# w_out loaded by column halves, and the first MoE2 chunk computed by column halves

## The chip, the cores and the metric

The kernel runs on one core of a Trainium2 chip. The metric is the device time of one execution in microseconds (us); lower is better.

## What is computed

Sliding-window attention with a linear bias, then a two-layer network with the activation h cos h:

```python
B, H, S, D = 8, 8, 576, 64                 # q, k, v: [B, H, S, D]
scores = q @ k^T / sqrt(D)
bias   = -slope[head] * |i - j|            # kept where 0 <= i - j < 128
x   = softmax(scores + bias) @ v           # as [B*S, H*D] = [4608, 512]
h   = x @ w_in                             # w_in  [512, 2048]
out = (h * cos(h)) @ w_out                 # w_out [2048, 512]
```

Inputs and output are float32 in HBM; inside, the kernel works in bfloat16 with float32 sums. Loads issued by GpSimd convert on the way, so that the sizes of loads in the profile are those of the bfloat16 that is written.

## The kernel before

The 4608 tokens are cut into nine chunks of 512 (`NCH` = 9). For a chunk, **MoE1** (`moe1`, L760) makes h in 16 feature blocks of 128 (`fc`): four matmuls each, a cosine on ScalarE (L765) and a product on VectorE (L769) that gives the tile `gT`. In chunk 0 the first blocks go by parts of 128 or 256 tokens (`moe1_part`, L784). **MoE2** (`moe2`, L813) then makes the output: for each of four token tiles of 128 rows, 16 matmuls over the feature blocks with 512 columns of `w_out` as the moving operand, summed in one PSUM bank. It has the two banks `OB` = [0, 1] in turn. ScalarE or VectorE copies the bank to `ob` (L820, L821), and SyncE's queue stores it (L825).

Between them runs the **attention** of the next tokens, in units: block 0 of a batch, then three blocks by two groups of heads, then a last block of 64. A unit has scores (L569), an exponential (L596), a mask on VectorE (L615), the product with V (L631 to L645), a division (L668 to L682), and the way into `xT`, which is the input of MoE1: by TensorE transposes (L722) or by a transposing DMA on SyncE's queue (L744, L747). After MoE1 of chunk 0, units 7 to 14 are due, in pairs: the last of batch 0 and seven of batch 1. The queries and keys of batches 0 and 1 are transposed on TensorE (L510), the later ones by DMAs on SyncE's queue (L412, L415).

**The loads** are issued by GpSimd (L384 q and k, L392 V, L403 later q and k, L424 w_in, L431 w_out), in the order in which they are written down. They pass through one queue, so that a load lands behind those issued before it. At the start that order is: rows of q and k, V of batch 0 and w_in, mixed; `qend` and `kend`, the last 64 tokens of batch 0's q and k; the last quarter of w_in; q and k of batch 1; the last V of batch 0; w_out in four pieces; V of batch 1 in five; then q and k of batch 2 in five pieces each (`qnat`, `knat`).

**The order on every engine** comes from a planner (`Plan.schedule`). Each operation is written with the time that it occupies its engine (`occ`), the time until its result is there (`lat`), a priority (`pri`, low goes first) and the keys that it reads and writes. For a load `lat` is the time that it takes on the wire, and the planner adds these up in the queue's order:

```python
wire = max(wire, st + 2300) + o.lat
o.end = max(wire, st + o.occ + 1400) + 500
```

From these times it writes out, before the kernel is built, which operation stands behind which on each engine; on the chip each engine follows that order and waits on semaphores. On TensorE an operation with a priority below 5 (scores, products with V, transposes) is taken when it can start; otherwise the one that can start first, and of those the lowest priority (MoE1 has 5, MoE2 has 6) and the earliest written:

```python
near = [(st, o) for st, o in cand if st <= soon]
return min(near, key=lambda c: (c[1].pri, c[1].seq))
```

A matmul of MoE2 reads the key `("wo", u)` of its piece of w_out: before the change piece u holds the rows of feature blocks 4u to 4u + 3 with all 512 columns.

Of the kernel before, what the change touches and what calls it, by code (L numbers as in the profile page):

```python
# [7 lines left out]
ACTF = mybir.ActivationFunctionType  # L8
# [3 lines left out]
B, H, S, D = 8, 8, 576, 64  # L12
# [5 lines left out]
NFC = DFF // 128  # L18
# [268 lines left out]
def bass_alibi_sliding__then__act_gcu_kernel(  # L287
# [8 lines left out]
    with ExitStack() as ctx:  # L296
# [4 lines left out]
        op = R.op  # L301
# [64 lines left out]
        def load_qk(which, src, b, n=0):  # L366
            t0, rr, _ = PIECES[b][n]
            c0 = 64 * (t0 // 32)
            rows = bass.AP(src.tensor, src[b].offset + 64 * t0,
                           [[64 * rr, 32], [64 * S, H], [1, 64 * rr]])  # L370
            if b == 0 and n == 0:
                op("sp" if which == "q" else "act", [lambda e: e.dma_start(qF[which][:, :, :], rows)],
                   w=[("qF", which)], dma=f"ld{which}f", occ=700 if which == "q" else 2000,
                   lat=4000 if which == "q" else 3300, pri=0)
                i = qF[which][:, :, :].rearrange("p y (j d) -> p y j d", j=4)
                o = qC[which][:, :, :, :].rearrange("p j y d -> p y j d")
                op(("act", "dve"),
                   {"act": lambda e: e.activation(o, i, ACTF.Copy),
                    "dve": lambda e: e.tensor_copy(o, i)},
                   r=[("qF", which)], w=piece_keys(which, b, n), occ={"act": 460, "dve": 330},  # L380
                   lat={"act": 560, "dve": 410}, pri=2)
                return
            o = qE[which][:, :, :] if t0 == 512 else qB[which][:, :, c0:c0 + 64 * rr]
            op("pool", [lambda e: e.dma_start(o, rows)],  # L384
               w=piece_keys(which, b, n), dma=f"ld{which}{n}", occ=750,
               lat={2: 600, 4: 800 if which == 'q' else 900,
                    8: 2600 if which == 'q' else 1300, 18: 2850}[rr])

        def load_v(b, order=range(NBLK), behind=()):
            for t in order:  # L390
# [32 lines left out]
        def load_w_in(f0, f1):  # L423
            op("pool", [lambda e: e.dma_start(  # L424
                w_in[:, :, 256 * f0:256 * f1],
                moe_w_in[:, 256 * f0:256 * f1].rearrange("(k p) c -> p k c", p=128))],
               w=[("wi", f) for f in range(f0, f1)], dma=f"wi{f0}", occ=750,
               lat=1300 * (f1 - f0))

        def load_w_out(u):  # L430
            op("pool", [lambda e: e.dma_start(  # L431
                w_out[:, 4 * u:4 * u + 4, :],
                moe_w_out[512 * u:512 * u + 512, :].rearrange("(f p) j -> p f j", p=128))],
               w=[("wo", u)], dma=f"wo{u}", occ=750, lat=2600)

        def constants():
            op("dve", lambda e: e.memset(zeros[:, :], 0.0), w=["zeros"], occ=60, pri=0)
# [364 lines left out]
        def moe2(c):  # L802
            gi = c % 2
            for t in range(4):
                tg = 4 * c + t
                last = tg == 4 * NCH - 1
                row = CH * c + 128 * t
                for n, (j0, j1) in enumerate([(0, 384), (384, 512)] if last else [(0, 512)]):
                    bank = OB[(tg + n) % 2]
                    oi = (tg + n) % NOB  # L810
                    w = j1 - j0
                    for fc in range(NFC):
                        op("pe", lambda e, t=t, fc=fc, bank=bank, j0=j0, j1=j1: e.matmul(  # L813
                            ps[:, bank, 0:j1 - j0], gT[gi][:, fc, 128 * t:128 * t + 128],
                            w_out[:, fc, j0:j1], start=(fc == 0), stop=(fc == NFC - 1)),
                           r=[("g", gi, fc, t), ("wo", fc // 4)], w=[("B", bank)],
                           occ=w * 427 // 1024 + 3, lat=w * 427 // 1024 + 166, pri=6)
                    o, i = ob[oi][:, 0:w], ps[:, bank, 0:w]
                    op(("act", "dve"),
                       {"act": lambda e, o=o, i=i: e.activation(o, i, ACTF.Copy),  # L820
                        "dve": lambda e, o=o, i=i: e.tensor_copy(o, i)},  # L821
                       w=[("B", bank), ("ob", oi)],
                       occ={"act": 70 + 420 * w // 512, "dve": 70 + 536 * w // 512},
                       lat={"act": 170 + 420 * w // 512, "dve": 155 + 536 * w // 512}, pri=6)
                    op("sp", [lambda e, o=o, row=row, j0=j0, j1=j1: e.dma_start(  # L825
                        out[row:row + 128, j0:j1], o)],
                       r=[("ob", oi)], dma=f"st{oi}", occ=350, lat=0)

        ucount = [0]

# [74 lines left out]
        load_qk("q", q, 1)  # L905
        load_qk("k", k, 1)
        load_v(0, [4])
        for u in range(4):
            load_w_out(u)
        load_v(1)  # L910
        next_t, next_v = 2, 2
        for c in range(NCH):
            if c == 0:
# [22 lines left out]
            while next_t < B and done >= 8 * (next_t - 1):  # L936
# [4 lines left out]
                if next_t < B:  # L941
                    load_nat("q", q, next_t)
                    load_nat("k", k, next_t)
            moe2(c)
        R.schedule(filler=lambda e: e.matmul(ps[:, UB[1], 0:128], zeros[:, :],
                                             zeros[:, :], start=True, stop=True),
                   fill=(900, 8300))
# [29 lines left out]
```

## Time and profile before

| | |
|---|---|
| median of 3 runs | 309.34 us (309.11 to 309.60) |
| the profiled execution | 309.74 us |
| its span, first to last instruction | 307.9 us |
| granted TensorE clock, mean | 1.00 |
| TensorE busy | 299.7 us |
| ScalarE, VectorE busy | 199.9, 194.1 us |

Times in the rows below are microseconds from the start of the span. PE is TensorE's matmuls, PEld its weight loads, DVE VectorE, ACT ScalarE, POOL GpSimd, SP SyncE; a q behind it is the engine's own queue. A row of the timeline has the start, the length, the engine and line, the operation, what it writes and reads, its shape and count; in brackets stands the idle time ahead of it and what ended it. A matmul's length is longer than its distance from the next, since they are pipelined. A row of the stages has the stretch, its length, and the busy time (instructions) of PE, PEld, DVE, ACT and POOL, then clock, DMA share and GB/s. A row of DMA issues has the kind, the count, the bytes written and the time from issue to landing. Some matmul records are missing from the trace.

### The profile page before, as it was taken

What the parts mean: (1) busy time and instruction counts of PE and PEld (TensorE: products, weight loads), DVE (VectorE), ACT (ScalarE), POOL (GpSimd) and SP (SyncE); (2) the same over time, 40 slices, a digit from 0 to 9 for tenths busy, and PEclk for the clock granted to TensorE, in tenths of its full rate; (3) what the DMA queues carried; (4) which work ended last, traced back from release to release, by engine and by line L of the source; (5) the groups of instructions that cost most, each with busy time, mean ns of one, the idle gap of its engine ahead of it and who ended that gap; (6) DMA issues with size and microseconds to landing.
All of it is one profiled execution on the core that took longest, in us unless ns stands there. A gap on an engine that the chain in (4) does not pass through costs nothing.

```text
span 307.9 us, 6411 instructions
## 1 busy us (share of the span) xinstructions
PE 299.7 (97%) x2556; PEld 157.4 (51%) x2600; DVE 194.1 (63%) x402; ACT 199.9 (65%) x268; POOL 97.0 (32%) x122
## 2 busy tenths in 40 slices
PE   8899999999999999999999999999999999999996
PEld 6685555445554555445544554455445554444444
DVE  6687777574668566856785568656966588742000
ACT  6888854885488746873688378746964588752211
POOL 8997201355055505550348023900500000000000
PEclk9999999999999999999999999999999999999999
DMA  9999999999399979999699959995991420001112
GB/s 148 173 204 207 207 162 203 140 162 181 105 127 130 170 122 141 129 168 106 155 122 156 151 109 150 165 179 96 169 106 44 113 70 0 0 0 70 68 73 97
DMA packets 150332, 39.08 MB, mean 127 GB/s; under 512 B 138912, under 2 KB 145312, under 8 KB 150304
## 3 DMA queue, kind: packets, MB, share of 16 engines
q0 software_dynamic: 100688, 18.10, 80.6%
q1 hardware_dynamic: 49344, 20.33, 33.2%
q8 instruction: 20, 0.33, 0.5%
q10 hardware_dynamic: 272, 0.26, 0.3%
q14 instruction: 8, 0.07, 0.1%
HBM read 36.70 MB, written 9.44 MB: 150 GB/s over the span
## 4 chain that ended last, share of the span: by engine, by line
PE 83%; DMA 7%; POOL 5%; ACT 2%; issue 1%; DVE 1%; POOLq 0%; ACTq 0%
PE ps L813 37%; PE ps L760 36%; DMA w_outb<-in_moe_w_out_dram 7%; PE ps L569 5%; ACT p L596 2%; PE ps L643 2%; PE ps L645 2%; POOL vp L392 1%; PE ps L631 1%; POOL w_inb L424 1%; POOL qrows L384 1%; POOL krows L384 1%; PE ps L635 1%; DVE p L615 1%; POOL w_outb L431 0%
## 5 line engine op out<-in xcount | busy, mean ns | idle before, releaser
L813 PE MATMUL ps<-w_outb,gT 128*128 128x512 bf16 (+2 forms) x566 | 132.8, 373 | 2.6 <-issue 1.1
L760 PE MATMUL ps<-xT,w_inb 128*128 128x512 bf16 x528 | 120.9, 379 | 0.9 <-issue 0.2
L769 DVE TENSOR_TENSOR gT<-ps,cos 128x512 bf16<-128x512 f32 x136 | 90.3, 688 | 21.1 <-ACT cos L765 16.3
L765 ACT ACTIVATE cos<-ps,halfpi 128x512 f32<-128x512 f32 x136 | 90.0, 688 | 18.9 <-PE ps L760 13.9
L596 ACT ACTIVATE p<-ps 128x1024 bf16<-128x1024 f32 x64 | 61.7, 1023 | 33.3 <-PE ps L569 33.3
L760 PEld LDWEIGHTS ps<-xT,w_inb 128*128 128x128 bf16 x544 | 52.0, 98 | 59.5 <-ACT p L596 0.6
L813 PEld LDWEIGHTS ps<-w_outb,gT 128*128 128x128 bf16 x592 | 53.2, 98 | 56.4 <-DMA w_outb<-in_moe_w_out_dram 1.7
L392 POOL DMA_DIRECT2D vp<-in_v_dram x40 | 33.7, 867 | 88.4 <-DMA xT<-xnat 68.9
L615 DVE TENSOR_TENSOR p<-p,emask 128x1024 bf16<-128x1024 bf16 x58 | 39.1, 682 | 26.8 <-ACT p L596 26.7
L820 ACT ACTIVATE ob<-ps 128x512 f32<-128x512 f32 (+2 forms) x21 | 12.1, 576 | 41.8 <-PE ps L813 35.3
L403 POOL DMA_DIRECT2D qnat<-in_q_dram x30 | 25.3, 876 | 23.1 <-DMA qt<-qnat 23.1
L403 POOL DMA_DIRECT2D knat<-in_k_dram x30 | 25.3, 874 | 11.1 <-DMA kt<-knat 8.3
L682 DVE TENSOR_TENSOR xnat<-ps,rec 128x256 bf16<-128x256 f32 x48 | 19.8, 420 | 1.3
L821 DVE COPY ob<-ps 128x512 f32<-128x512 f32 x16 | 10.9, 683 | 15.1 <-PE ps L813 15.1
L569 PE MATMUL ps<-qt,kt 64*128 64x128 bf16 (+1 forms) x576 | 19.4, 211 | 0.4 <-DVE qt L526 0.2
L569 PEld LDWEIGHTS ps<-qt,kt 64*128 64x128 bf16 x576 | 14.5, 94 | 9.7 <-issue 4.5
L643 PEld LDWEIGHTS ps<-vp,p 128*128 128x128 bf16 x192 | 14.2, 97 | 9.0 <-issue 6.1
L643 PE MATMUL ps<-vp,p 128*128 128x65 bf16 x192 | 17.4, 193 | 0.2 <-ACT xT L731 0.2
L645 PE MATMUL ps<-vp,p 128*128 128x65 bf16 x192 | 17.5, 193 | 0.0
L645 PEld LDWEIGHTS ps<-vp,p 128*128 128x128 bf16 x192 | 13.2, 97 | 2.3
L680 DVE RECIPROCAL rec<-ps 128x4 f32<-128x4 f32 x48 | 8.2, 176 | 6.3 <-PE ps L645 5.8
L631 PEld LDWEIGHTS ps<-vp,p 128*128 128x128 bf16 x128 | 7.3, 97 | 3.6 <-issue 1.8
(66 smaller groups left out, 150.0 us busy)
## 6 DMA issues: line engine op xcount, KB each, us to landing
out_dram<-ob SPq DMA_DIRECT2D x35, 256.0 KB, 2.2
vp<-in_v_dram POOLq DMA_DIRECT2D x32, 128.0 KB, 7.1
qnat<-in_q_dram POOLq DMA_DIRECT2D x24, 128.0 KB, 6.6
knat<-in_k_dram POOLq DMA_DIRECT2D x24, 128.0 KB, 5.1
w_outb<-in_moe_w_out_dram POOLq DMA_DIRECT2D x4, 512.0 KB, 21.9
w_inb<-in_moe_w_in_dram POOLq DMA_DIRECT2D x3, 512.0 KB, 12.8
qrows<-in_q_dram POOLq DMA_DIRECT2D x1, 576.0 KB, 15.6
krows<-in_k_dram POOLq DMA_DIRECT2D x1, 576.0 KB, 17.7
```

The source lines that it names most:

```text
L392: op("pool", [lambda e, t=t, rows=rows: e.dma_start(vp[b % 2][0:rows, t, :, 0:64], v[b, :, 128 * t:128 * t + rows, :].rearrange("h p d -> ...
L403: fns.append(lambda e, t=t, rows=rows: e.dma_start(nat[which][0:rows, t, :, :], src[b, :, 128 * t:128 * t + rows, :].rearrange("h p d -> p ...
L569: ins = e.matmul(ps[:, banks[x], c0:c0 + n_], keys_ap(b, x, pr, kc), query_ap(b, x, pr, qb, n_), start=not acc, stop=stop)
L596: op("act", lambda e: e.activation(P[i][:, 0:1024], ps[:, banks[0]:banks[0] + 2, :].rearrange("p a b -> p (a b)"), ACTF.Exp, scale=0.125), ...
L615: op("dve", lambda e: e.tensor_tensor(p, p, m, ALU.mult), r=[("P", i), ("EM", 0), ("EM", 1)], w=[("P", i)], occ=600, lat=690, pri=1)
L643: e.matmul(o, P[i][:, c0:c0 + 128], V[:, qb - 1, h, 0:65], start=True, stop=False)
L645: ins = e.matmul(o, P[i][:, c0 + 128:c0 + 256], V[:, qb, h, 0:65], start=False, stop=True)
L682: op("dve", lambda e: e.tensor_tensor(o, U[:, :, :, 0:64], rv[:, :, :, None].broadcast_to([128, 2, 2, 64]), ALU.mult), r=[("rec", n % 4)], ...
L760: op("pe", lambda e, kc=kc: e.matmul(ps[:, bank, :], w_in[:, kc, 128 * fc:128 * fc + 128], xT[:, kc, r0:r0 + CH], start=(kc == 0), stop=(k ...
L765: op("act", lambda e: e.activation(cosb[ci][:, :], ps[:, bank, :], ACTF.Sin, bias=halfpi[:, 0:1]), r=["halfpi"], w=[("B", bank), ("cos", c ...
L769: op("dve", lambda e: e.tensor_tensor(gT[gi][:, fc, :], ps[:, bank, :], cosb[ci][:, :], ALU.mult), r=[("cos", ci)], w=[("B", bank)] + [("g ...
L813: op("pe", lambda e, t=t, fc=fc, bank=bank, j0=j0, j1=j1: e.matmul(ps[:, bank, 0:j1 - j0], gT[gi][:, fc, 128 * t:128 * t + 128], w_out[:, ...
```

## The change

w_out is loaded in four pieces again, but each has half of the columns and half of the rows: pieces 0 and 1 are columns 0 to 255 for feature blocks 0 to 7 and 8 to 15, pieces 2 and 3 the same for columns 256 to 511. V of batch 1 is loaded between the second and the third piece. MoE2 of chunk 0 is written by column halves (`moe2_first`): for each half the four token tiles in the order 0, 2, 1, 3, with 16 matmuls of 256 columns each. Tiles 0 and 1 share bank 0, tiles 2 and 3 bank 1, one in each half of it. A full bank is copied out at once and stored as 256 rows by 256 columns. The other chunks keep `moe2`, where a matmul now waits for both column halves of its rows. Planned times of loads that are not otherwise changed are lowered: `qend` and `kend` from 600 to 370 ns, q and k of batch 1 from 2850 to 2790, w_in from 1300 to 1275 for each 256 columns. The time planned for issuing a piece of w_out goes from 750 to 900.

```diff
-               lat={2: 600, 4: 800 if which == 'q' else 900,
-                    8: 2600 if which == 'q' else 1300, 18: 2850}[rr])
+               lat={2: 370, 4: 800 if which == 'q' else 900,
+                    8: 2600 if which == 'q' else 1300, 18: 2790}[rr])
...
-               lat=1300 * (f1 - f0))
+               lat=1275 * (f1 - f0))
 
         def load_w_out(u):
+            f0, j0 = 8 * (u % 2), 256 * (u // 2)
             op("pool", [lambda e: e.dma_start(
-                w_out[:, 4 * u:4 * u + 4, :],
-                moe_w_out[512 * u:512 * u + 512, :].rearrange("(f p) j -> p f j", p=128))],
-               w=[("wo", u)], dma=f"wo{u}", occ=750, lat=2600)
+                w_out[:, f0:f0 + 8, j0:j0 + 256],
+                moe_w_out[128 * f0:128 * f0 + 1024, j0:j0 + 256].rearrange(
+                    "(f p) j -> p f j", p=128))],
+               w=[("wo", u)], dma=f"wo{u}", occ=900, lat=2600)
...
-                           r=[("g", gi, fc, t), ("wo", fc // 4)], w=[("B", bank)],
+                           r=[("g", gi, fc, t), ("wo", fc // 8), ("wo", 2 + fc // 8)], w=[("B", bank)],
...
+        def moe2_first():
+            for y in range(2):
+                j0 = 256 * y
+                for t in (0, 2, 1, 3):
+                    for fc in range(NFC):
+                        op("pe", lambda e, t=t, fc=fc, j0=j0: e.matmul(
+                            ps[:, OB[t // 2], 256 * (t % 2):256 * (t % 2) + 256],
+                            gT[0][:, fc, 128 * t:128 * t + 128], w_out[:, fc, j0:j0 + 256],
+                            start=(fc == 0), stop=(fc == NFC - 1)),
+                           r=[("g", 0, fc, t), ("wo", 2 * y + fc // 8)], w=[("B", OB[t // 2])],
+                           occ=109, lat=275, pri=6)
+                for n, bank in enumerate(OB):
+                    oi = 2 * y + n
+                    o = ob[oi][:, :]
+                    i = ps[:, bank, :]
+                    op(("act", "dve"),
+                       {"act": lambda e, o=o, i=i: e.activation(o, i, ACTF.Copy),
+                        "dve": lambda e, o=o, i=i: e.tensor_copy(o, i)},
+                       w=[("B", bank), ("ob", oi)], occ={"act": 490, "dve": 606},
+                       lat={"act": 590, "dve": 691}, pri=6)
+                    o = out[256 * n:256 * n + 256, j0:j0 + 256].rearrange("(t p) j -> p t j", p=128)
+                    i = ob[oi][:, :].rearrange("p (t j) -> p t j", t=2)
+                    op("sp", [lambda e, o=o, i=i: e.dma_start(o, i)],
+                       r=[("ob", oi)], dma=f"st{oi}", occ=400, lat=0)
...
-        for u in range(4):
-            load_w_out(u)
+        load_w_out(0)
+        load_w_out(1)
         load_v(1)
+        load_w_out(2)
+        load_w_out(3)
...
-            moe2(c)
+            moe2_first() if c == 0 else moe2(c)
```

## The prediction

> **What bounds the kernel now.** I read the page first: the busy line, the granted clock and the chain that ended last.
>
> ```profile
> span 307.9 us, 6411 instructions
> PE 299.7 (97%) x2556; PEld 157.4 (51%) x2600; DVE 194.1 (63%) x402; ACT 199.9 (65%) x268; POOL 97.0 (32%) x122
> PEclk9999999999999999999999999999999999999999
> PE 83%; DMA 7%; POOL 5%; ACT 2%; issue 1%; DVE 1%; POOLq 0%; ACTq 0%
> ```
>
> TensorE is busy for 97% of the span at full granted clock, so only its idle time can be won, and work added to it is paid. The one large share of the chain that is not TensorE's is 7% of DMA. The table by stages says how much idle time there is around the change, and the chain in order of time says what the 7% is:
>
> ```profile
> 54.00:300.00 246.00, 243.47 (x1872) 121.21 (x1908) 155.39 (x304) 159.36 (x211) 65.89 (x79) 1.00 1.10 115
> 34.40:54.05 19.65, 18.73 (x216) 10.31 (x219) 13.11 (x34) 11.89 (x17) 1.33 (x2) 1.00 1.90 188
> ```
> ```profile
> 16.56 22.84 DMA w_outb<-in_moe_w_out_dram
> ```
>
> The first number after the comma is TensorE's busy time. In the stage in which MoE2 of chunk 0 runs it is idle for 19.65 - 18.73 = 0.92 us; in all of 54 to 300 us for 2.5 us. A gain above 0.9 us has no source in this stage. The chain passes through the third piece of w_out, which lands at 39.40: up to there TensorE waits on the load queue, from there on it only works. TensorE's timeline shows the same:
>
> ```profile
> 34.44 1.89 PE L813 MATMUL ps<-w_outb,gT 128*128 128x512 bf16 x8
> 36.42 0.63 PE L569 MATMUL ps<-qt,kt 64*128 64x64 bf16 x24
> 36.98 1.90 PE L813 MATMUL ps<-w_outb,gT 128*128 128x512 bf16 x8
> 39.45 1.04 PE L813 MATMUL ps<-w_outb,gT 128*128 128x512 bf16 x4 [0.56 <-DMA w_outb<-in_moe_w_out_dram]
> 54.04 13.98 PE L760 MATMUL ps<-xT,w_inb 128*128 128x512 bf16 x63
> ```
>
> Eight matmuls of the first piece (two token tiles by four row blocks), the scores of two units, eight of the second piece, then 0.56 us of idle until the third. From 39.45 to 54.04, where chunk 1's MoE1 begins, no wait is left that matters. So the number to find is: when does the last wait for w_out end after the change, and how much MoE2 work is left then? All before that wait is hidden by it; all behind it is paid.
>
> **When the pieces land.** Issues on GpSimd's queue, and time to landing of the four pieces of w_out in order and of the first piece of V behind them:
>
> ```profile
> 15.08 2.99 POOL L431 DMA_DIRECT2D w_outb<-in_moe_w_out_dram  x4
> 18.03 4.24 POOL L392 DMA_DIRECT2D vp<-in_v_dram  x5
> ```
> ```profile
> w_outb<-in_moe_w_out_dram POOLq DMA_DIRECT2D x1, 512.0 KB, 19.2
> w_outb<-in_moe_w_out_dram POOLq DMA_DIRECT2D x1, 512.0 KB, 21.0
> w_outb<-in_moe_w_out_dram POOLq DMA_DIRECT2D x1, 512.0 KB, 22.8
> w_outb<-in_moe_w_out_dram POOLq DMA_DIRECT2D x1, 512.0 KB, 24.8
> vp<-in_v_dram POOLq DMA_DIRECT2D x1, 128.0 KB, 24.9
> ```
>
> The issues are 0.75 us apart, so the pieces land at 34.3, 36.83, 39.4 and 42.1, and V at 42.9: one queue, in order, 2.54 us for a piece of w_out and 0.8 for 128 KB of V. Nothing ahead of w_out is changed, so its first piece still starts at 31.74.
>
> A piece after the change is as many bytes, but 1024 rows of 512 bytes as written in place of 512 rows of 1024. What the packets cost, from two stretches of the trace: one in which the queue moves the 512-byte rows of q and k (4.3 to 5.3 us), one in which it moves w_out (32 to 38 us):
>
> ```profile
> DMA packets 385, 0.19 MB, mean 187 GB/s; under 512 B 26, under 2 KB 385, under 8 KB 385
> DMA packets 1246, 1.24 MB, mean 207 GB/s; under 512 B 36, under 2 KB 1246, under 8 KB 1246
> ```
>
> Without the small ones that is 359 packets of 512 bytes a us (352 on this queue, which I take) against 1210/6 = 202 of 1024 bytes. A new piece takes 1024/352 = 2.91 us, an old one 512/202 = 2.54: 0.37 us more for each. The second piece, with which the first column half is complete, lands at 36.83 + 2 x 0.37 = 37.57.
> The Trainium skill says in DMA: Bandwidth & Descriptors, under Specifications, that transfers of 512 bytes and more run at line rate. By that the second piece would land at 36.83 and the sum below come out at 0.0; the 187 against 207 GB/s of the two rows disagrees. The same page of the Trainium skill, under Why small descriptors are slow, gives every packet about 3 cycles beside one for each 32 bytes: 2 x 19 / 35, an estimate of 9% more time, and a sum of about +0.4 us; the two rows have 15%.
>
> **Part by part.** First, what the order makes of it. The order on TensorE is fixed beforehand by the planner from planned landing times. The diff lowers those of loads that it doesn't touch: eight steps of w_in by 25 ns, two loads by 230, two by 60, together 780 ns up to w_out. The real queue doesn't get faster, and the order of today fits it: the second group of L813 starts at 36.98, right after the landing at 36.83. So work that needs a load goes up to 0.8 us too early into TensorE's in-order queue. The first place is the transposes of qend and kend, which today are let go by kend itself:
>
> ```profile
> 23.30 0.14 PEld L510 LDWEIGHTS ps<-ident,qend 128*64 128x64 bf16 x4 [0.22 <-DMA kend<-in_k_dram]
> ```
>
> Their planned landing moves by 6 x 25 + 2 x 230 = 610 ns; I expect two matmul groups to go behind them and TensorE to stand there for some 0.65 us. Behind it everything on TensorE, MoE1 of chunk 0 and its cosines on ScalarE included, is that much later, and MoE2 begins at 35.1 and not 34.44. This isn't added to the sum, since the wait for the second piece swallows it.
>
> Second, that wait. With the first piece (rows of blocks 0 to 7, half the columns) tile 0 has eight matmuls of 256 columns and tile 2 eight more. The planner picks the oldest that is ready, and goes back to tile 0's blocks 8 to 15 as soon as the second piece is planned to be in, 0.78 us earlier than now, at about 36.0. From 34.44 on, eight half matmuls (0.9 us) and the scores (36.42 to 36.98, and the switch, 0.7) reach that point, so about 2 of tile 2 come ahead: 10 of 128 are done when TensorE stands at 35.1 + 1.1 + 0.7 = 36.9, and it waits to 37.57. The number of 10 can be 8 to 16, 0.1 us each.
>
> Third, the work left. A matmul of 512 columns is issued every (1.89 - 0.38)/7 = 0.216 us (first row of the timeline above; 379 ns is one by itself). For 256 columns there are those of MoE1's parts:
>
> ```profile
> L813 PE MATMUL ps<-w_outb,gT 128*128 128x512 bf16 x534 | 129.3, 379 | 2.6 <-issue 1.1 <-DMA w_outb<-in_moe_w_out_dram 0.6
> L784 PE MATMUL ps<-xT,w_inb 128*128 128x256 bf16 x32 | 4.1, 273 | 0.0
> ```
> ```profile
> 23.65 1.48 PE L784 MATMUL ps<-xT,w_inb 128*128 128x256 bf16 x12
> ```
>
> (1.48 - 0.273)/11 = 0.1097, 0.109 to 0.110 with the rounding: twice as many matmuls and weight loads cost 0.1 to 0.2 us in all. Before: TensorE goes on at 39.45 with 64 - 16 = 48 matmuls left, 10.36 us; together 49.81. After: at 37.57 + 0.05 with 118 left, 12.9 us; together 50.5. The attention work left is the same in both, one pair of scores being done. **The sum: +0.7 us.**
>
> Fourth, the rest at nothing. V of batch 1 between the halves lands from 38.4 instead of 42.9; TensorE's weight loads wait for V by 0.7 us in the whole kernel, and its users need exponentials first:
>
> ```profile
> PEld ps L643 <- DMA vp<-in_v_dram: 0.5, 1, 0.5
> PEld ps L631 <- DMA vp<-in_v_dram: 0.2, 1, 0.2
> ```
>
> The second half lands at 37.57 + 3.6 (V) + 2.91 = 44.1 and at 47.0. Until 44.1 TensorE has 54 more half matmuls (5.9 us) and attention; for the last piece see the rival. Four evictions of 128x512 and four stores of 256 KB stay as many; the stores' rows are shorter, behind nothing that TensorE needs. On GpSimd the extra descriptors are covered by loads that wait 20 us in the queue. What is behind them, q and k of batch 2, comes 4 x 0.37 = 1.5 us later, and their transposes on SyncE's queue with them:
>
> ```profile
> 31.69 1.56 POOL L403 DMA_DIRECT2D knat<-in_k_dram  x2 [2.61 <-issue]
> 57.91 5.98 SPq L412 DMA_TRANSPOSE kt<-knat  x1
> 63.93 1.25 SPq L415 DMA_TRANSPOSE kt<-knat  x1
> 71.19 0.85 PE L569 MATMUL ps<-qt,kt 64*128 64x64 bf16 x32
> ```
> ```profile
> knat<-in_k_dram POOLq DMA_DIRECT2D x1, 64.0 KB, 24.9
> kt<-knat SPq DMA_TRANSPOSE x1, 4.9
> ```
>
> The last piece of k lands at 57.4, the last transposed tile at 68.8, and the scores that need it run at 71.19. 1.2 to 1.5 us later is still 0.9 us ahead of them; with that gone, each us would cost a us.
>
> **The rivals.** *Slower still: the last piece of w_out becomes the wait.* It is planned at 2.6 us behind the third and takes 2.91, with transposes and stores of SyncE's queue beside it. Packets on the load queue in 44 to 46, 46 to 48 and 48 to 50 us today:
>
> ```profile
> q0 software_dynamic: 2449, 0.31, 242.3%
> q0 software_dynamic: 1924, 0.24, 189.2%
> q0 software_dynamic: 1542, 0.19, 151.9%
> ```
>
> Beside those transfers (525 + 907) packets of 2449 per 2 us are lost: 1.2 us. The piece then lands at 48.2. TensorE asks for it after half 0 (7 us from 35.1, the 0.7 of waiting) and some 4 us of attention and half 1's first blocks, at about 47.2. Where it does so earlier than 48.2, each us is a us: up to +1.0 more, +1.7, 311.0 us.
> *No change: a new piece takes 2.54 us like an old one, or 16 matmuls go ahead of the wait.* The first: 36.9 + 12.9 - 49.8 = 0.0; the second: 37.62 + 112 x 0.109 - 49.81 = 0.0; 309.3. The 352 packets a us speak against the first, the planner's rule against the second. (The Trainium skill's line rate, above, is the first.)
> *Faster: the order puts enough ahead of every w_out wait.* Attention could begin earlier, since V does, and fill the place of the 0.56 us. All 0.92 us of idle time gone, less 0.15 for the shorter matmuls: -0.8, 308.6. For it: a column half gives 64 matmuls (7 us) at once at 37.57, where three pieces of rows give 24 of 512 columns (5.2 us) up to 42.1. Against it: the wait for the second piece is no shorter than the one removed, and the planned times are 0.8 us too early.
>
> **How the numbers follow.** The profiled execution took 309.74 us, 1.84 outside its span, 0.40 above the median of 309.34; I add to the median: 309.34 + 0.7 = 310.0. A measurement can tell about 0.2% here, 0.62 us: 308.72 to 309.96. Forecast 0.38 (its own range 309.6 to 310.4, 0.22 above the bound, 0.16 inside); last piece late 0.22 (slower); no change 0.14 (same); faster 0.26 (0.24 past the bound, 0.02 inside). Faster 0.24, same 0.32, slower 0.44. The range from 308.7 to 311.1 leaves out most of the fully faster case and the tail above.
>
> **What would show it.** TensorE waits on kend at 22.6 to 23.3; MoE2's first matmul near 35.1; a wait for w_out of 0.3 to 0.8 us that ends near 37.6; V landing from 38.4; the last pieces near 44 and 47; MoE1 of chunk 1 with some matmuls of chunk 0's MoE2 left behind it. I am wrong where the second piece lands before 37.0, where no wait stands at 37, or where one over 0.3 us stands behind it.

## The result and the profile after

The changed kernel takes 310.12 us (median of 18 runs, 309.48 to 311.14), the kernel before, run beside it, 309.58 us (18 runs, 308.87 to 310.07). The ratio is 1.0021, with a 95% interval of 1.0011 to 1.0030: slower by about 0.5 us, where 0.7 was forecast. The profiled execution took 310.58 us, 0.84 more than that of before. The first lines of the page, and the shares of the chain that ended last:

```profile
span 308.8 us, 6544 instructions
PE 300.1 (97%) x2623; PEld 163.4 (53%) x2664; DVE 193.7 (63%) x402; ACT 200.7 (65%) x268; POOL 97.5 (32%) x122
PE 83%; DMA 8%; POOL 3%; ACT 2%; issue 1%; DVE 1%; SPq 0%; POOLq 0%; ACTq 0%
```

TensorE is busy 0.4 us longer, and the chain's DMA share has grown from 7 to 8%. So transfers still set part of the end. Which ones is seen on TensorE's timeline:

```profile
23.28 0.30 PE L513 MATMUL ps<-ident,qend 128*64 128x128 bf16 x4 [0.39 <-DMA kend<-in_k_dram]
...
35.01 2.02 PE L838 MATMUL ps<-w_outb,gT 128*128 128x256 bf16 x17
36.96 0.63 PE L572 MATMUL ps<-qt,kt 64*128 64x64 bf16 x24
37.52 3.45 PE L838 MATMUL ps<-w_outb,gT 128*128 128x256 bf16 x30
...
53.32 0.49 PE L838 MATMUL ps<-w_outb,gT 128*128 128x256 bf16 x3
54.46 13.76 PE L763 MATMUL ps<-xT,w_inb 128*128 128x512 bf16 x62 [0.65 <-DMA xT<-xfirst]
...
120.76 0.82 PE L763 MATMUL ps<-xT,w_inb 128*128 128x512 bf16 x3 [0.23 <-DMA xT<-xnat]
```

No matmul of MoE2 of chunk 0 (L838) waits for w_out any more. In the place of that wait there are three others: for kend at 22.9, for the DMA transpose of xfirst at 53.8, just ahead of MoE1 of chunk 1 (L763), and a small one at 120.5. The table by stages shows the exchange, above before and below after (third number: TensorE's busy time):

```profile
35.00:54.00 19.00, 18.08 (x213) 1.00 1.92 187
54.00:90.00 36.00, 35.69 (x287) 1.00 1.45 143
```
```profile
35.00:54.00 19.00, 18.81 (x277) 1.00 1.90 175
54.00:90.00 36.00, 35.17 (x282) 1.00 1.37 152
```

In the stage of the change TensorE's idle time falls from 0.92 to 0.19 us. In the next one it rises from 0.31 to 0.83 us.

What a wait costs is read from the step between two matmuls, since the idle time in brackets is shorter by the overlap of a matmul with the next. What goes: before, the second group of L813 began at 36.98 and the third at 39.45; eight matmuls of 0.216 us are 1.73 of these 2.47 us, so the wait cost 0.74 us. Two smaller waits of the kernel before go with it, 0.16 us ahead of the scores at 36.42 and 0.08 us at 28.2 (0.98 in all). What comes: kend 0.46 (the step to its transposes takes 0.61 us, and 0.15 where kend is there in time); xfirst 54.46 - 53.32 = 1.14 less three half matmuls (0.33), 0.81; the wait at 120 us 0.39 (a step of 0.60 less 0.216); the half-width matmuls 0.16 (below); and 0.19 us by which this execution was already behind at 17 us, after waits for its first loads. The sum is -0.98 + 0.46 + 0.81 + 0.39 + 0.16 + 0.19 = +1.03 us. The two profiled executions differ by 0.84, so that the account closes to 0.2 us.

### The profile page after: what moved, and what is told of

Read it like the earlier page. It is cut to its first block, busy times and chain, and to the rows that moved or that the text cites. A ratio compares the mean times of both kernels' runs of the same rounds, so it can differ in the third digit from the quotient of the medians.

```text
span 308.8 us, 6544 instructions
## 1 busy us (share of the span) xinstructions
PE 300.1 (97%) x2623; PEld 163.4 (53%) x2664; DVE 193.7 (63%) x402; ACT 200.7 (65%) x268; POOL 97.5 (32%) x122
## 4 chain that ended last, share of the span: by engine, by line
PE 83%; DMA 8%; POOL 3%; ACT 2%; issue 1%; DVE 1%; SPq 0%; POOLq 0%; ACTq 0%
PE ps L763 38%; PE ps L816 32%; PE ps L572 4%; DMA kend<-in_k_dram 4%; DMA xT<-xfirst 3%; PE ps L838 3%; ACT p L599 2%; DMA xT<-xnat 1%; PE ps L646 1%; PE ps L634 1%; PE ps L648 1%; POOL vp L392 1%; POOL w_inb L424 1%; PE ps L513 1%; PE ps L787 1%
## 5 line engine op out<-in xcount | busy, mean ns | idle before, releaser
L763 PE MATMUL ps<-xT,w_inb 128*128 128x512 bf16 x527 | 121.0, 379 | 1.7 <-DMA xT<-xfirst 0.6
L816 PE MATMUL ps<-w_outb,gT 128*128 128x512 bf16 (+2 forms) x506 | 117.2, 372 | 1.9 <-issue 1.1
L763 PEld LDWEIGHTS ps<-xT,w_inb 128*128 128x128 bf16 x544 | 51.7, 98 | 60.6 <-DMA xT<-xnat 0.7
L816 PEld LDWEIGHTS ps<-w_outb,gT 128*128 128x128 bf16 x528 | 47.8, 98 | 50.1
L823 ACT ACTIVATE ob<-ps 128x512 f32<-128x512 f32 (+2 forms) x19 | 10.9, 574 | 41.1 <-PE ps L816 34.4
L824 DVE COPY ob<-ps 128x512 f32<-128x512 f32 x14 | 9.6, 683 | 15.1 <-PE ps L816 15.1
L646 PEld LDWEIGHTS ps<-vp,p 128*128 128x128 bf16 x192 | 14.2, 97 | 8.1 <-issue 5.0
L838 PE MATMUL ps<-w_outb,gT 128*128 128x256 bf16 x128 | 16.1, 273 | 0.0
L648 PEld LDWEIGHTS ps<-vp,p 128*128 128x128 bf16 x192 | 13.2, 97 | 2.5
L838 PEld LDWEIGHTS ps<-w_outb,gT 128*128 128x128 bf16 x128 | 11.8, 98 | 1.9
## 6 DMA issues: line engine op xcount, KB each, us to landing
w_inb<-in_moe_w_in_dram POOLq DMA_DIRECT2D x3, 512.0 KB, 11.9
```

The costliest lines, as they stand in the source:

```text
L646: e.matmul(o, P[i][:, c0:c0 + 128], V[:, qb - 1, h, 0:65], start=True, stop=False)
L648: ins = e.matmul(o, P[i][:, c0 + 128:c0 + 256], V[:, qb, h, 0:65], start=False, stop=True)
L763: op("pe", lambda e, kc=kc: e.matmul(ps[:, bank, :], w_in[:, kc, 128 * fc:128 * fc + 128], xT[:, kc, r0:r0 + CH], start=(kc == 0), stop=(k ...
L838: op("pe", lambda e, t=t, fc=fc, j0=j0: e.matmul(ps[:, OB[t // 2], 256 * (t % 2):256 * (t % 2) + 256], gT[0][:, fc, 128 * t:128 * t + 128] ...
```

## The experiments

The theory to test was that the change does remove the waits for w_out, and that other loads, whose landing times it does not improve, become waits in their place: kend, because the planner's figures for it were lowered, and xfirst, because the column halves finish both banks at once and two stores go ahead of it. The rivals were that the halves themselves cost the time, that the lowered figures cost it through the order, or that the place of V does; a later one was that any other set of figures reshuffles the order after 100 us and that this costs. Ratios are against the kernel before, run beside each experiment (its median was 309.44 to 309.56).

### One store behind xfirst

```diff
-        def moe2_first():
+        def moe2_first(behind):
...
-                       r=[("ob", oi)], dma=f"st{oi}", occ=400, lat=0)
+                       r=[("ob", oi)], dma=f"st{oi}", occ=400, lat=0,
+                       after=behind if oi == 1 else ())
...
-            moe2_first() if c == 0 else moe2(c)
+            moe2_first(begin) if c == 0 else moe2(c)
```

> The changed kernel with one thing moved: the second store of the first column half is issued behind the transposing DMA of xfirst instead of ahead of it. The order on TensorE, ScalarE and VectorE stays exactly the same. Theory A (the changed kernel loses its time at 53.8 us, where MoE1 of chunk 1 waits for xfirst, because two stores and no longer one pass through SyncE's ring ahead of it): xfirst lands some 2 us sooner, near 52.4 instead of 54.3, the 0.65 us of idle time ahead of MoE1 goes, and the kernel takes 0.6 to 0.8 us less than the changed one, 309.4 or a little below. Theory B (the time is lost to the half-width matmuls and the planner's earlier figures, and the wait only shows it): within 0.2 us of the changed kernel, 310.1.

Measured: 309.92 us (11 runs), ratio 1.0013 (0.9998 to 1.0027). SyncE's queue in the changed kernel, and behind it the time in us that xfirst took from issue to landing:

```profile
43.96 1.31 SPq L855 DMA_DIRECT2D out_dram<-ob  x2
45.32 1.41 SPq L747 DMA_TRANSPOSE xT<-xfirst  x1
```
```profile
xT<-xfirst SPq DMA_TRANSPOSE x1, 8.9
```

and with the second store behind it:

```profile
44.02 0.58 SPq L855 DMA_DIRECT2D out_dram<-ob  x1
45.30 1.27 SPq L747 DMA_TRANSPOSE xT<-xfirst  x1
46.62 0.61 SPq L855 DMA_DIRECT2D out_dram<-ob  x1
```
```profile
xT<-xfirst SPq DMA_TRANSPOSE x1, 7.8
```

The gain of 0.6 to 0.8 us that Theory A expected did not come: the time is 0.2 us below the changed kernel's, which the two intervals do not tell apart. The transpose is issued at the same time and lands 1.1 us earlier, at 53.1 in place of 54.2, and the wait list of this kernel has none for it. One store less ahead of it is the only difference in SyncE's order. But other waits came in:

```profile
22.95 0.30 PE L513 MATMUL ps<-ident,qend 128*64 128x128 bf16 x4
...
34.75 2.34 PE L838 MATMUL ps<-w_outb,gT 128*128 128x256 bf16 x17
37.02 0.63 PE L572 MATMUL ps<-qt,kt 64*128 64x64 bf16 x24
...
46.62 0.61 PE L838 MATMUL ps<-w_outb,gT 128*128 128x256 bf16 x4 [0.31 <-DMA w_outb<-in_moe_w_out_dram]
```

In this execution kend landed 11.4 us after its issue and not 11.7, so nothing waited for it and MoE2 began at 34.75, 0.26 us earlier. The scores nevertheless begin at 37.02, where the changed kernel had 36.96: the 17th matmul stood for the second piece of w_out. And the last piece of w_out is late by 0.47 us (from 45.93, two matmuls before, to 46.62, less 0.22). The moved store is not the cause of that: the third piece had already landed 0.8 us later than in the changed kernel (43.95 against 43.12), before the first of these stores was issued.

### xfirst transposed by TensorE

```diff
-(4 if phase else 2)
+(4 if phase else 1)
```

> The changed kernel with the 128 tokens of xfirst transposed by TensorE (as in the first phase) instead of by a DMA on SyncE's queue. Theory A: no wait at 53.8 us, so 0.6 to 0.8 us are won; four transposes and two more evictions cost about 0.3 us; in sum 0.3 to 0.5 us below the changed kernel, 309.7. Theory B: 0.3 us above the changed kernel, 310.4.

Measured: 310.52 us (5 runs), 1.0035 (1.0021 to 1.0048). The wait for xfirst is gone here as well, and w_out is waited for in two places:

```profile
36.72 0.28 PE L838 MATMUL ps<-w_outb,gT 128*128 128x256 bf16 x1 [0.17 <-DMA w_outb<-in_moe_w_out_dram]
46.78 0.39 PE L838 MATMUL ps<-w_outb,gT 128*128 128x256 bf16 x2 [0.59 <-DMA w_outb<-in_moe_w_out_dram]
```

By the step they cost 0.33 and 0.75 us. The time is the one that Theory B gave, but these waits, and not the mechanism of Theory B, are what the trace shows. Here too the last two pieces of w_out landed about 1 us later than in the changed kernel (44.1 and 46.7 against 43.1 and 45.8). With the transposes now on the engine that bounds the kernel, removing the wait in this way gained nothing.

### The planner's figures alone, in both directions

The changed kernel with the old figures:

```diff
-               lat={2: 370, 4: 800 if which == 'q' else 900,
-                    8: 2600 if which == 'q' else 1300, 18: 2790}[rr])
+               lat={2: 600, 4: 800 if which == 'q' else 900,
+                    8: 2600 if which == 'q' else 1300, 18: 2850}[rr])
...
-               lat=1275 * (f1 - f0))
+               lat=1300 * (f1 - f0))
```

> The changed kernel with the planner's figures of before (600, 2850 and 1300 ns). Theory A: the wait for kend at 23 us (0.39 us of idle time) goes, MoE2 begins near 34.6 instead of 35.0, and its w_out pieces land at 34.0 and 36.6, in time; xfirst is issued 0.4 us sooner as well but still behind two stores, so the wait for it stays: 0.3 to 0.5 us below the changed kernel, 309.7. Theory C (the figures don't matter, since a wait further on takes the time up again): no difference from the changed kernel, 310.1.

Measured: 310.78 us (6 runs), 1.0047 (1.0032 to 1.0062). The wait for kend is gone, as expected, and MoE2 begins at 33.98, a full us earlier (0.64 us of it stood already at 17 us, where TensorE's order is still the same and waits for the first rows of q and k differ between executions). The time did not fall by the 0.3 to 0.5 us that I had expected; it lies above what both theories gave. The same wait for xfirst stands at the end of the stage (0.44 idle), and the order after 100 us, which the planner now makes otherwise, has waits of 0.41 at 119.3 us, for a DMA transpose of x, and 0.33 at 209.9 us, where a product with V waits for the mask on VectorE.

The kernel before with the new figures, and nothing else:

```diff
-               lat={2: 600, 4: 800 if which == 'q' else 900,
-                    8: 2600 if which == 'q' else 1300, 18: 2850}[rr])
+               lat={2: 370, 4: 800 if which == 'q' else 900,
+                    8: 2600 if which == 'q' else 1300, 18: 2790}[rr])
...
-               lat=1300 * (f1 - f0))
+               lat=1275 * (f1 - f0))
```

> The kernel before with only the planner's figures changed (370, 2790 and 1275 ns); loads and matmuls as they were. Theory A: TensorE waits 0.4 to 0.6 us for kend at 23 us, but the wait for the third piece of w_out, which ends at 39.4 whatever comes before, gets shorter by as much: within 0.2 us of the kernel before, 309.6. Theory D (the figures alone are what the change costs): 0.4 to 0.6 us above it, 310.1.

Measured: 309.84 us (11 runs), 1.0010 (0.9999 to 1.0022). This cannot be told from the kernel before; Theory A's 309.6 lies nearer than Theory D's 310.1. All four pieces of w_out are the old ones, by rows, and yet the exchange is the same as in the changed kernel:

```profile
23.13 0.25 PE L510 MATMUL ps<-ident,qend 128*64 128x128 bf16 x2 [0.32 <-DMA kend<-in_k_dram]
...
54.73 1.47 PE L760 MATMUL ps<-xT,w_inb 128*128 128x512 bf16 x6 [0.54 <-DMA xT<-xfirst]
```

The wait for w_out is gone, kend costs 0.39 us (0.32 of it idle), and xfirst 0.70 (1.13 from the group before less two matmuls). SyncE's queue tells why. The kernel before, and behind it this run:

```profile
43.95 0.36 SPq L825 DMA_DIRECT2D out_dram<-ob  x1
45.41 1.24 SPq L744 DMA_TRANSPOSE xT<-xfirst  x1
```
```profile
xT<-xfirst SPq DMA_TRANSPOSE x1, 6.9
```
```profile
44.84 1.04 SPq L825 DMA_DIRECT2D out_dram<-ob  x2
45.92 1.34 SPq L744 DMA_TRANSPOSE xT<-xfirst  x1
```
```profile
xT<-xfirst SPq DMA_TRANSPOSE x1, 8.8
```

The kernel before had one store between the transposes of xtail and xfirst, and xfirst landed after 6.9 us. Here the order puts two there, without column halves, and it takes 8.8.

### V behind all four pieces

```diff
         load_w_out(1)
-        load_v(1)
         load_w_out(2)
         load_w_out(3)
+        load_v(1)
```

> The changed kernel with V of batch 1 loaded behind all four pieces of w_out, as before the change. Theory A: V comes 5.3 us later, near 42.5, as it did before; TensorE has column half 0 to work on until about 44, so that the wait for V stays under 0.5 us; xfirst is made 0.5 to 1 us later, and MoE1 of chunk 1 waits that much longer for it: 0.3 to 0.8 us above the changed kernel, 310.4 to 310.9. Theory G (V between the halves is what costs, since it makes the last pieces of w_out late): 0.3 us or more below it, 309.8.

Measured: 310.47 us (10 runs), 1.0033 (1.0021 to 1.0046). This was measured together with the changed kernel once more:

> The changed kernel once more, for a second profile of it, since the landing times of the load queue differ by up to 0.5 us between profiles. Theory A (new waits for kend and for xfirst stand in the place of the wait for w_out): together 0.7 to 1.3 us of idle time at 23 and at 54 us again, no wait for w_out over 0.3 us, 310.1. Theory F (the waits of the first profile were an accident of its landing times, and the loss is elsewhere): other places.

Measured: 310.54 us (12 runs, 309.60 to 311.37), 1.0031 (1.0018 to 1.0044). So the place of V makes no difference that can be told here. More is to be learnt from the profile of the repeated kernel: it took 309.71 us, 0.87 less than the first profile of the same program, and is one of the fastest of these 12 runs. Its one wait of note up to 60 us is

```profile
PE ps L513 <- DMA kend<-in_k_dram: 0.3, 1, 0.3
```

and for xfirst, which landed 8.5 us after its issue, it loses 0.26 us (53.09 to 53.68, less 0.33):

```profile
53.09 0.49 PE L838 MATMUL ps<-w_outb,gT 128*128 128x256 bf16 x3
53.68 2.55 PE L763 MATMUL ps<-xT,w_inb 128*128 128x512 bf16 x11
```

By the step kend costs 0.33 us here; the wait at 120 us is 0.09, and the execution was 0.03 us behind at 17 us. The account is -0.98 + 0.33 + 0.26 + 0.09 + 0.16 + 0.03 = -0.11 us, and the measured difference of the profiled executions -0.03. The same order cost 0.8 us in one execution and nothing in the other, by some tenths of a us in three landings.

### Column halves in seven more chunks of the kernel before

```diff
+                    cuts = [(0, 256), (256, 512)] if 0 < c < 8 else [(j0, j1)]
+                    for a0, a1 in cuts:
+                        for fc in range(NFC):
...
+                                w_out[:, fc, a0:a1], start=(fc == 0), stop=(fc == NFC - 1)),
```

> The kernel before, with MoE2 of chunks 1 to 7 by column halves inside the same bank: 16 matmuls of the left 256 columns, then 16 of the right, 448 more matmuls and weight loads, no change in loads, evictions and stores. All theories: 448 times 1.5 to 3.5 ns (0.109 to 0.1097 us for a half against 0.216 / 2), so 0.7 to 1.6 us above the kernel before, 310.3 to 311.2; that makes 0.1 to 0.2 us for the 64 more of the change. If it is 3 us or more above, the half-width matmuls are the change's cost by themselves.

Measured: 311.60 us (6 runs), 1.0069 (1.0054 to 1.0083), some 2.1 us more, past the expected range. Back to back, one half follows the other after 109.15 ns on average and one whole matmul the other after 215.81, so a pair costs 2.5 ns more than the whole it replaces, and 448 pairs 1.1 us. The rest has a name too: a wait of 0.64 us for a DMA transpose of x at 185.5, in an order that the planner made anew. Together they are some 1.8 us, and the profiled execution took 311.56, 1.82 more than that of before; the wait for w_out (0.6) is still there in it. By the 2.5 ns, the 64 pairs of the change cost 0.16 us.

### One wait taken away, then several

The expectations of these runs also speak of the order after 100 us, which came out otherwise in the run with the old figures. First, the store behind xfirst and the planned landing of w_out raised by 100 ns:

```diff
-               w=[("wo", u)], dma=f"wo{u}", occ=900, lat=2600)
+               w=[("wo", u)], dma=f"wo{u}", occ=900, lat=2700)
```

> The changed kernel with the second store of the first half behind the transposing DMA of xfirst, and with 2700 instead of 2600 ns planned for a piece of w_out (2.67 us is what the pieces were apart in the changed kernel's trace), so that the scores go ahead of the matmul that needs the second piece. Theory A: no wait for xfirst and less than 0.3 us for w_out in sum, kend as in the changed kernel: 0.4 to 0.8 us below the changed kernel, 309.3 to 309.7. Theory E (the order that the planner makes further on, which any change of its figures reshuffles, decides by as much): between 309.9 and 310.8, with the waits at 36 and 46 us gone but 0.3 to 0.9 us of new ones behind 100 us, as in the kernel with the old figures.

Measured: 310.65 us (8 runs), 1.0040 (1.0027 to 1.0054). This is the time that Theory E gave. The early waits are small (kend 0.34, w_out 0.24 at 36.9 and at 46.06), but in the order after 100 us two waits stand as in the run with the old figures, 0.31 at 119.7 and 0.35 at 210.2. A figure changed for one load moves work 160 us later.

Second, a change of figures chosen so that TensorE's order differs in the two transpose groups of qend and kend alone:

```diff
-               lat={2: 370, 4: 800 if which == 'q' else 900,
+               lat={2: 600, 4: 800 if which == 'q' else 900,
...
-               lat=1275 * (f1 - f0))
+               lat=1275 * (f1 - f0) - (460 if f0 == 6 else 0))
```

> The changed kernel with 600 instead of 370 ns planned for qend and for kend, and the 460 ns taken off the last piece of w_in, so that all planned landings behind it stay. The only difference in the order is that the transposes of qend and kend stand two matmul groups (0.66 us) later on TensorE, as before the change. Theory A: the wait for kend of 0.3 to 0.5 us at 22.5 us goes, TensorE comes to MoE2 that much earlier, near 34.6, and waits there for the second piece of w_out (0.2 to 0.4 us at 36 to 37) and again for xfirst at 54 us: it wins nothing, within 0.25 us of the changed kernel. Theory H (each wait on TensorE is paid in full): 0.3 to 0.5 us below the changed kernel.

Measured: 310.44 us (12 runs), 1.0027 (1.0013 to 1.0041). The wait for kend is gone and nothing is won against the changed kernel's 310.12 and 310.54, as Theory A had it. The profile, at 311.09 us one of the longer executions, shows what was next:

```profile
PE ps L787 <- DMA w_inb<-in_moe_w_in_dram: 0.7, 1, 0.7
PE ps L763 <- DMA xT<-xfirst: 0.5, 1, 0.5
PE ps L513 <- DMA qrows<-in_q_dram: 0.2, 1, 0.2
PE ps L838 <- DMA w_outb<-in_moe_w_out_dram: 0.2, 1, 0.2
```

Third, the store behind xfirst and V in two parts, so that the last two pieces of w_out have less V ahead of them:

```diff
         load_w_out(1)
-        load_v(1)
+        load_v(1, [0, 1])
         load_w_out(2)
         load_w_out(3)
+        load_v(1, [2, 3, 4])
```

> The changed kernel with the second store of the first half behind the transposing DMA of xfirst, and with only the first two pieces of V between the column halves, the other three behind them. The orders on TensorE, ScalarE and VectorE stay the same. Theory A: the last piece of w_out lands 1.9 us sooner, near 44.7, so that neither xfirst nor it is waited for; what stays is kend (0.3 to 0.5 us) or, where kend lands early, the second piece: 0.5 to 0.9 us below the changed kernel, 309.3 to 309.9, about the kernel before. Theory E (the order further on decides): no difference from the changed kernel, since that order is the same.

Measured: 309.88 us (12 runs), 1.0009 (0.9995 to 1.0023). Neither xfirst nor the last piece of w_out is waited for; kend (0.33), the second piece (0.35 at 36.1) and a transpose of x (0.45 at 119.4) are.

Last, all of it together: the late store, V in two parts, the figures of the run for kend, and the second piece of w_out planned 200 ns later and the third 200 ns earlier.

```diff
-               w=[("wo", u)], dma=f"wo{u}", occ=900, lat=2600)
+               w=[("wo", u)], dma=f"wo{u}", occ=900, lat=2600 + {1: 200, 2: -200}.get(u, 0))
```

> All mended at once, with the order further on left as it is: transposes of qend and kend two groups later, the second store behind xfirst's DMA, two pieces of V between the halves and three behind them, and 200 ns more planned for the second piece of w_out (200 less for the third), so that the scores go ahead of the matmul that needs the second piece. Theory A: under 0.3 us of waits between 14 and 57 us, against 0.9 in the kernel before; less 0.17 us for the half-width matmuls this is 0.4 to 0.6 us below the kernel before, 308.9 to 309.2, and 1.0 us or more below the changed one. If the waits go and the time is no better than the kernel before, the idle time ahead of 57 us is not what decides.

Measured: 309.28 us (12 runs), 0.9990 (0.9977 to 1.0002). Again, on another chip:

> The kernel with everything mended once more, for a second profile and a second interval. Theory A: again under 0.3 us of waits between 14 and 57 us, and 0.2 to 0.6 us below the kernel before, 309.0 to 309.3. If the first result was chance: within 0.2 us of the kernel before on either side, or waits for xfirst, kend or w_out over 0.3 us.

Measured: 309.61 us (12 runs), 1.0006 (0.9995 to 1.0017). The timeline of the first of the two:

```profile
34.33 1.91 PE L838 MATMUL ps<-w_outb,gT 128*128 128x256 bf16 x16
36.17 0.63 PE L572 MATMUL ps<-qt,kt 64*128 64x64 bf16 x24
36.87 3.45 PE L838 MATMUL ps<-w_outb,gT 128*128 128x256 bf16 x30
...
52.67 0.49 PE L838 MATMUL ps<-w_outb,gT 128*128 128x256 bf16 x3
53.21 2.97 PE L763 MATMUL ps<-xT,w_inb 128*128 128x512 bf16 x13
```

Between 17 and 60 us no matmul waits for a transfer by more than 0.14 us here. The first matmul of MoE1 of chunk 1 is missing from this trace; its weights are loaded at 52.95, so that it begins at 53.0, some 1.5 us earlier than in the changed kernel. Both ratios lie below the changed kernel's 1.0021 and 1.0031, the first of them clear of those intervals, so the new waits together are what the change costs. But the two results straddle the kernel before (0.27 us below it and 0.05 above), and the gain that Theory A expected of both runs did not come: with all the new waits mended, the change is worth nothing that can be told from nothing.

### All accounts together

In this table a wait is what the step from one matmul to the next takes beyond the usual step of its kind, wherever that is 0.08 us or more. Where a step is longer by just one matmul of 512 columns, and the weights of that matmul are seen to be loaded, its record is missing from the trace, and the step is no wait. "Behind at 17 us" is how much later than in the kernel before the execution has come to the matmul of MoE1 that stands at 16.81 there; waits for the first loads decide it. The sum adds this and the waits, takes off the 0.98 us of waits that the kernel before has behind 17 us, and adds 0.16 us for the half-width matmuls where the kernel has them (1.1 us in the run with halves in seven more chunks). Beside it stands the execution's own time less the 309.74 us of before.

| kernel | behind at 17 us | waits in us | sum | measured |
|---|---|---|---|---|
| changed | 0.19 | kend 0.46, xfirst 0.81, at 120 us 0.39 | +1.03 | +0.84 |
| changed, again | 0.03 | kend 0.33, xfirst 0.26, at 120 us 0.09 | -0.11 | -0.03 |
| one store later | 0.32 | w_out 0.31 and 0.47, at 120 us 0.10 | +0.38 | +0.51 |
| old figures | -0.45 | xfirst 0.60, at 119 us 0.41, at 210 us 0.33, four others 0.48 | +0.55 | +0.63 |
| before, new figures | 0.11 | kend 0.39, xfirst 0.70 | +0.22 | +0.23 |
| V behind | -0.11 | kend 0.33, w_out 0.63, xfirst 0.51, at 120 us 0.39, two others 0.18 | +1.11 | +1.17 |
| halves in seven more chunks | -0.11 | w_out 0.78, at 185.5 us 0.64, three others 0.35 | +1.79 | +1.82 |
| w_out planned later | -0.22 | kend 0.34, w_out 0.24 and 0.24, at 120 us 0.31, at 210 us 0.35, three others 0.34 | +0.78 | +0.95 |
| kend alone | -0.22 | w_in 0.85, qrows 0.30, w_out 0.32, xfirst 0.62, at 120 us 0.48 | +1.53 | +1.35 |
| V in two parts | -0.21 | kend 0.33, w_out 0.35, at 119 us 0.45 | +0.10 | +0.17 |
| all mended | -0.10 | w_out 0.14, qrows 0.10 | -0.68 | -0.66 |
| all mended, again | 0.05 | qrows 0.34, at 17 us 0.14 | -0.29 | -0.27 |

The sums meet the measured differences to 0.2 us in all twelve. So TensorE's waits, most of them for transfers, account for the differences between these kernels, as far as single executions show it. The run with xfirst on TensorE is left out, since nothing measures what its transposes cost there. Not every wait was set by itself.

## Why the prediction was right or wrong

The time came out within 0.12 us of the forecast and the sign is right; against the kernel before it is 0.5 us, and 1.1 us in the repeat, where 0.7 was forecast. The steps behind it were right in part only, and that the number agrees is in good part luck.

- **The wait for kend**: right. It was expected at 22.6 to 23.3 with some 0.65 us, and stands at 22.9 to 23.28 with 0.39 idle, 0.46 by the step. MoE2 began at 35.01, where 35.1 was forecast; 0.19 of the 0.57 us by which it is later than before stood already at 17 us, so that this agreement is in part chance. That this wait is worth nothing by itself was also right: with kend early MoE2 began 0.26 us earlier and the scores at the same time, and the run that moves those two groups alone won nothing.
- **The landing of the second piece**: wrong; this is the term that was mis-sized. The prediction took 352 packets of 512 bytes a us and 2.91 us for a piece. The first two pieces landed at 34.0 and 36.6, 2.6 us apart, and not at 37.57. In the eleven profiles with such pieces the median distance is 2.66 us, against 2.54 for the old pieces:

```profile
15.06 1.77 POOL L433 DMA_DIRECT2D w_outb<-in_moe_w_out_dram  x2
```
```profile
w_outb<-in_moe_w_out_dram POOLq DMA_DIRECT2D x1, 512.0 KB, 18.9
...
w_outb<-in_moe_w_out_dram POOLq DMA_DIRECT2D x1, 512.0 KB, 20.7
```
```profile
DMA packets 1172, 0.59 MB, mean 197 GB/s; under 512 B 17, under 2 KB 1172, under 8 KB 1172
```

  The last row is 31 to 34 us of the changed kernel: (1172 - 17)/3 = 385 packets a us, by which 1024 take 2.66. The 352 came from one us at 4.3 to 5.3, in the start of the kernel, and did not hold for this longer transfer. The rate makes 0.5 of the 0.96 us by which the piece came early. The queue was also ahead (the load in front of w_out landed at 31.56 and not at 31.83), and the rest is not accounted for; over the eleven profiles the second piece landed at 36.2 to 37.3, never as late as 37.57. The rule that the prediction weighed against it, line rate from 512 bytes on (the Trainium skill, DMA: Bandwidth & Descriptors, Specifications), comes nearer than the row: a piece takes 5% longer, where that rule has nothing, the prediction's estimate from cycles a packet had 9%, and the row taken had 15%.
- **The matmuls ahead of the wait**: wrong. All 16 that the first piece allows ran ahead of it, and not 10; the piece landed as they ended, and the forecast wait of 0.7 us near 37 does not exist. The prediction had said that it would be wrong where the second piece lands before 37.0 or no wait stands at 37. Both happened. This is what its rival of no change describes: 16 matmuls ahead, and a piece that takes nearly as long as an old one.
- **The work left**: right. The halves cost 0.16 us, and 0.1 to 0.2 was forecast.
- **The rest at nothing**: wrong in one place, and that place gave the time. Of the stores the prediction said that they "stay as many" and stand "behind nothing that TensorE needs"; it did not ask what TensorE needs from behind them. They are as many, but two of them now go out together ahead of the transpose of xfirst on SyncE's queue, and MoE1 of chunk 1 loses 0.81 us to it. The rest of that part held: V landed in time, and the scores of batch 2 run at 71.61 (71.19 before) without a wait for it.
- **The last piece of w_out as the wait**: not in the changed kernel, but in the two in which the wait for xfirst was taken away by itself, with 0.31 and 0.59 us of idle time. In both the third piece had landed 0.8 us or more later than in the changed kernel, so it was the spread of landings, and not the edit, that brought the wait out. The rival was real, and close.

So the number is right by another sum. The forecast had the wait for the second piece as the one that counts, and kend's wait hidden behind it. In the changed kernel TensorE, held up by kend, comes to the second piece only after it has landed, so that the time lost to kend stands in the place of a wait at 37, and a wait for xfirst that was not foreseen comes behind it.

What stays open: why one store less ahead brings xfirst from 8.9 to 7.8 us and not to the 6.9 of before (the store that is left has rows of half the length, and other loads land beside it; neither was tested by itself); what sets the landing times apart between executions of one program; what the waits at 119 and 210 us cost by themselves; and whether the mended version gains anything.

## What to carry to other kernels

Where loads follow each other through one queue and TensorE needs each of them just in time, a wait that is removed can uncover the next, and the new order can make others: list all loads that land within some tenths of a us of their use, and price the change by the last of them. Finishing two results at once puts two stores ahead of whatever that queue issues next, so look for what stands behind a store before calling it free. And take a packet's price from a long transfer of that kind, not from a short stretch of the start.

## What the runs showed of the hardware

- Rows of 512 bytes, as written, cost little: 2.66 us for 512 KB where rows of 1024 bytes take 2.54.
- A DMA transpose on SyncE's queue takes longer to land by what is ahead of it: that of xfirst took 8.5 to 8.9 us in six profiles with two stores of 256 KB directly ahead. With one store ahead it took 6.9 and 7.0 us in the two profiles where the store is 128 rows of 512 columns, and 7.7 to 7.9 in the five where it is 256 rows of 256 columns.
- Landing times of one load vary between executions by some tenths of a us (kend 11.7 and 11.4 us after its issue in two profiles of the changed kernel, 10.8 to 11.9 in all these profiles). That is as much as the change is worth, and makes two profiles of the same program differ by 0.87 us.
- A matmul of 256 columns follows the last after 109.15 ns, one of 512 after 215.81: halving costs 2.5 ns for each pair. The Trainium skill (TensorE: Matmul & The Clock Gate, Back-to-back issue gap) gives 2.5 ns for each matmul beside its columns at the full clock, and says that a stream of matmuls of 512 columns with their weight loads comes closer together, at 131 ns. By the first the distances would be 109.2 and 215.8 ns, and these agree; the second does not.
